# Laying out q and k of 14 attention chunks in DRAM for 32x32 turns on VectorE, with stores on SyncE's queue and GpSimd's long sums in halves

## The chip, the cores and the metric

The kernel runs on one core of one Trainium2 chip. Its time is the device time of one execution in microseconds (us); the figure to be predicted is the median of several runs. A core has five engines with an instruction stream each: TensorE (PE in the profile; its weight loads, PEld, are listed apart), VectorE (DVE), ScalarE (ACT), GpSimd (POOL) and SyncE (SP), which here only issues transfers. Transfers are carried out by 16 DMA engines, which serve a queue of SyncE (q1 in the profile) and one of ScalarE (q10).

## The reference

A linear attention with decay over blocks of the sequence, and after it a dense mixture of four two-layer networks. All is fp32.

```python
B, H, S, D = 4, 8, 768, 64            # q, k, v: (B, H, S, D)
for b in range(nb):                   # blocks of the sequence, kv_state starts at 0
    intra = einsum('bhic,bhjc->bhij', qb, kb) * Dmask
    intra = einsum('bhij,bhjd->bhid', intra, vb)
    inter = einsum('bhid,bhde->bhie', qb * lam_pow, kv_state)
    out[:, :, sl] = intra + inter
    kv_state = lam_block * kv_state + einsum('bhsd,bhse->bhde', kb * rev_pow, vb)
x = out.transpose(0, 2, 1, 3).reshape(B * S, H * D)       # (3072, 512)
p = domain_probs / (domain_probs.sum(-1, keepdims=True) + 1e-09)
for e in range(4):                    # w1: (4, 512, 1024), w2: (4, 1024, 512)
    h = maximum(x @ w1[e], 0.0)
    y += p[:, e:e + 1] * (h @ w2[e])
```

The kernel works in chunks of 128 positions: 6 for each of the 4 batches, 24 in all, numbered n = 0 to 23. The products of the mixture are cut in Strassen's way, with seven products (M1 to M7) where eight blocks would stand, on two levels; that takes sums and differences of blocks, which VectorE and GpSimd form.

## The kernel before

The scores need q and k with the feature on the partitions, and DRAM has them with the position on the partitions. A chunk is loaded in its natural layout, turned by TensorE against an identity, four transposes for q and four for k, and copied out of PSUM by ScalarE. VectorE scales q, GpSimd scales k in place once it is turned.

```python
def load(n, names="qkv"):
    b, c = divmod(n, NCH)                                   # NCH = 6 chunks in a batch
    for name in names:
        x = small(f"{name}n")                               # [128, 512], one of 47 buffers
        src = {"q": q, "k": k, "v": v}[name][b, :, c * C:(c + 1) * C, :]
        ...                                                 # q and k: two loads of 64 columns a head

def turn(n, tags):
    qn, kn = nat.pop((n, "q")), nat[n, "k"]
    qp, kp = bank(tags[0], "qp"), bank(tags[1], "kp")
    for x, y in ((qp, qn), (kp, kn)):
        for ac in range(NHP):                               # 4
            nc.tensor.transpose(out=x[:, ac * C:(ac + 1) * C], in_=y[:, 2 * ac:2 * ac + 2]..., identity=ident[:])
    qT, kT, qs = small("qT"), small("kT"), None
    nc.scalar.copy(out=qT[:], in_=qp[:])
    nc.scalar.copy(out=kT[:], in_=kp[:])
    if n % NCH:
        qs = small("qs")
        soon(n, lambda: tt(nc.vector, qs[:], qT[:], q_decay[:]..., ALU.mult))
    turned[n] = qT, kT, qs
    if n % NCH < NCH - 1:
        tt(nc.gpsimd, kd, kd, by.to_broadcast([P, NHP, 2, D]), ALU.mult)      # kd: kn, in place
```

`soon` puts small steps in front of a list of steps in the background, of which one is taken at each call of `rest()`. Chunks 0 to 7 are handled in an opening stage, the rest between the products of the mixture:

```python
for i in range(CPG + 2):                                    # opening: 8 chunks, first plain products
    ...
    for f, lag in ((scores, 1), (turn, 0), (values, 2)):
        ...
    if i + 4 < CPG:
        load(i + 4)
...
for at, (g, e) in enumerate(units):                         # 12 units: 3 groups of tokens, 4 experts
    for i in range(7):                                      # M1 .. M7
        ...
        for x, part in enumerate(order):                    # 8 parts: first product of the next unit,
            for f in part:                                  # second product of this one, in turns
                if f:
                    f()
            now[0] += 1
            ...
            rest()                                          # one step in the background
            if x == 0 and at * 7 + i >= 6 and fill:
                feed(*fill.pop(0))                          # loads xs_in, ws_in of a later product
            if steps and (at > 0 or i > 1) and (x == 5 or (x == 2 and i in (1, 3, 5) and at > 0)):
                steps.pop(0)()                              # turn, scores or values of one chunk
            if x % (2 if g == 0 else 3) == 0:
                pump()                                      # stores made before, then one chore
```

The operands of the products are summed by GpSimd, stored in DRAM and loaded again. Stores are issued by ScalarE, two pumps after they were noted:

```python
stores.append(lambda: (
    nc.scalar.dma_start(out=to[:, 0], in_=blk[:, 0, 0:256]),
    nc.scalar.dma_start(out=to[:, 1:5], in_=s[:]),
    nc.scalar.dma_start(out=to[:, 5:7], in_=blk[:, 1]...),
    made.add(what),
))

def total(name, a, b, op):                                  # of w1; w2 and x alike
    t = stage.tile([P, 2, W], FP32, name="w1o", tag="st")
    tt(nc.gpsimd, t[:], st[a][:], st[b][:], op)             # 1024 elements on each partition
    st[name] = t
```

Of the kernel before, what the change touches and what calls it, by code (L numbers as in the profile page):

```python
# [11 lines left out]
ALU = mybir.AluOpType  # L12
# [9 lines left out]
def kernel(  # L22
# [70 lines left out]
    def tt(eng, o, a, b, op):  # L93
        eng.tensor_tensor(out=o, in0=a, in1=b, op=op)  # L94


    nat = {}

    def load(n, names="qkv"):

        b, c = divmod(n, NCH)
        for name in names:
            x = small(f"{name}n")
            src = {"q": q, "k": k, "v": v}[name][b, :, c * C:(c + 1) * C, :]
            if name == "v":
                nc.sync.dma_start(out=x[:].rearrange("p (h d) -> p h d", d=D), in_=src.rearrange("h p d -> p h d"))
# [4 lines left out]
            nat[n, name] = x[:].rearrange("p (h d) -> p h d", d=D)  # L111

    lam_bc = consts.tile([P, H], FP32, name="lam_bc")
    nc.scalar.dma_start(out=lam_bc[:], in_=lam.partition_broadcast(P))
# [30 lines left out]
    def inner(eng, what, to, blk, ops, at):  # L145

        b = {n: blk[:, i, j * 256:(j + 1) * 256] for n, (i, j) in at.items()}
        s = stage.tile([P, 4, 256], FP32, name="ops", tag="st")
        for i, (name, x, y, op) in enumerate(ops):
            b[name] = s[:, SLOT[name]]  # L150
            tt(eng, b[name], b[x], b[y], op)
        stores.append(lambda: (
            nc.scalar.dma_start(out=to[:, 0], in_=blk[:, 0, 0:256]),
            nc.scalar.dma_start(out=to[:, 1:5], in_=s[:]),
            nc.scalar.dma_start(out=to[:, 5:7], in_=blk[:, 1].rearrange("p (a f) -> p a f", a=2)),
            made.add(what),
        ))

# [53 lines left out]
    def prepare_w2(e):  # L212
        st = {}

        def block(name, i, j):
            t = stage.tile([P, 2, 2, DH], FP32, name="w2b", tag="st")
            for uu in range(2):
                nc.sync.dma_start(out=t[:, uu], in_=w2_block(e, uu, i, j))
            st[name] = t

        def total(name, n, a, b, op):
            t = stage.tile([P, 2, 2, DH], FP32, name="w2o", tag="st")
            flat = [x[:].rearrange("p u c d -> p (u c d)") for x in (t, st[a], st[b])]
            tt(nc.gpsimd, *flat, op)
            stores.append(lambda: (
                nc.scalar.dma_start(out=w2_sums[e, n].rearrange("p u w -> p (u w)"), in_=flat[0]),
                made.add(("w2", e, name)),
            ))
# [32 lines left out]
    def prepare_w2_ops(e):  # L261
        st = {}

        def block(name, i, j):
            t = stage.tile([P, 2, 2, DH], FP32, name="w2b", tag="st")
            src = moe_w2[e, j * W:(j + 1) * W, i * DH:(i + 1) * DH]
            nc.sync.dma_start(out=t[:].rearrange("p q c d -> p (q c) d"), in_=src.rearrange("(k p) d -> p k d", p=P))
            st[name] = t

        def total(name, a, b, op):  # L270
            t = stage.tile([P, 2, 2, DH], FP32, name="w2o", tag="st")
            tt(nc.gpsimd, *(x[:].rearrange("p q c d -> p (q c d)") for x in (t, st[a], st[b])), op)
            st[name] = t

        return weight_steps(block, total, lambda m: inner_w2(e, m, st[A_OF[m]]))
# [8 lines left out]
    def prepare_x(g):  # L284

        st = {}

        def total(name, a, b, op):
            t = stage.tile([P, 2, W], FP32, name="xo", tag="st")
            tt(nc.gpsimd, t[:], a, b, op)  # L290
# [129 lines left out]
    def soon(n, *work):  # L420

        background[0:0] = work
        if n < CPG:
            rest(len(work))

    def turn(n, tags):
        qn, kn = nat.pop((n, "q")), nat[n, "k"]
        qp = bank(tags[0], "qp")
        kp = bank(tags[1], "kp")
        for x, y in ((qp, qn), (kp, kn)):  # L430
            for ac in range(NHP):
                nc.tensor.transpose(  # L432
                    out=x[:, ac * C:(ac + 1) * C], in_=y[:, 2 * ac:2 * ac + 2].rearrange("p r d -> p (r d)"),
                    identity=ident[:],
# [6 lines that stand above are left out]
            soon(n, lambda: tt(nc.vector, qs[:], qT[:], q_decay[:].rearrange("p h c -> p (h c)"), ALU.mult))  # L441
        turned[n] = qT, kT, qs
        if n % NCH < NCH - 1:

            kd = kn.rearrange("p (ac r) d -> p ac r d", r=2)
            by = k_decay.rearrange("p r ac -> p ac r").unsqueeze(3)
            tt(nc.gpsimd, kd, kd, by.to_broadcast([P, NHP, 2, D]), ALU.mult)

    def scores(n, tags):
        qT, kT, _ = turned[n]  # L450

        sp = [bank(tags[r], "sp") for r in range(2)]
# [57 lines left out]
    def attention(g):  # L510
# [3 lines left out]
        for n in range(g * CPG, (g + 1) * CPG):  # L514
# [3 lines left out]
            def end(n=n):  # L518
                values(n, ("s0", "s1"))
                if n + AHEAD < B * NCH:  # L520
                    load(n + AHEAD)
# [218 lines left out]
    def second_product(g, e, m, banks):  # L740

        def part(sj, s):
# [27 lines left out]
            else:  # L770
                nc.vector.scalar_tensor_tensor(out=o, in0=x, scalar=w, in1=o, op0=ALU.mult, op1=ALU.add)  # L771
            if e == E - 1 and m in ("M2", "M4", "M5", "M3"):
                stores.append(lambda: nc.scalar.dma_start(out=out[n * P:(n + 1) * P, j * DH:(j + 1) * DH], in_=o))

        def done():
            del fed2[g, e, m]
# [215 lines left out]
    def keep_own(what, to, pieces):  # L992
        def store():
            for (x, y), of in pieces:
                nc.scalar.dma_start(out=to[:, x:y], in_=of)
            made.add(what)

        stores.append(store)
# [47 lines left out]
    for i in range(CPG + 2):  # L1046
# [10 lines left out]
        for f, lag in ((scores, 1), (turn, 0), (values, 2)):  # L1057
# [16 lines left out]
    mine = {m: lambda m=m: own(m) for m in SEQ}  # L1074
    raws = [lambda n=n: raw_w1(1, n) for n in ("A11", "A12", "A21", "A22")]
    chores.extend((*prepare_w2(1), *raws, nothing, mine["M1"], lambda: sum_w1(1, "S1", "A21", "A22", ALU.add)))
    for m in SEQ0[2:]:
        for x, f in enumerate(direct_product(0, m, blocks, ("g1", "g3", "q01", "q02", "q11", "q12"))):
            f()
            rest()  # L1080
            if x < 4:
                pump()
    def sum_own(name, a, b):
# [14 lines left out]
    after_last = {"M2": (None,) * 5 + (("M3", 0), ("M3", 1)), "M4": (("M5", 0), ("M5", 1), ("M2", 0), ("M2", 1), ("M4", 0))}  # L1098
    steps = attention(1)
    for at, (g, e) in enumerate(units):  # L1100
        if (g, e) == (0, 1) or (g, e) == (0, 2):
            chores.extend(prepare_w2(e + 1) + prepare_w1((e + 2) % E))
        ahead = units[at + 1] if at + 1 < len(units) else None
# [9 lines left out]
        for i in range(7):  # L1113
# [27 lines left out]
            for x, part in enumerate(order):  # L1141
# [15 lines left out]
                        give(*y, ("s0", "s1"))  # L1157
                if x == 0 and at * 7 + i >= 6 and fill:
                    feed(*fill.pop(0))
                if at == 0 and x == 0 and i < AHEAD:  # L1160
# [35 lines left out]
```

## Time and profile before

The time is 1215.12 us, the median of 3 runs from 1214.82 to 1217.88 us. The profiled execution spans 1211.4 us at a granted TensorE clock of 0.999.

| what | value |
|---|---|
| q and k turned on TensorE (qp, kp) | 96 + 96 transposes of 128x128 |
| copies of qT and kT on ScalarE | 24 at 586 ns, 24 at 594 ns |
| q scaled on VectorE (qs) | 20 at 1184 ns |
| k scaled on GpSimd (kn) | 20 at 1074 ns |
| GpSimd sums of 128x1024 that the change cuts (w2o, w1o, xo) | 52, of 2.35 to 2.52 us in the mean of each group |
| loads of q and k, 128 KB each | 48 + 48, landing in 4.5 and 4.1 us |
| packets in all, bytes | 227446, 317.93 MB |
| packets under 512 B | 91648 |

The page of the profile has six parts: busy time of each engine; the same in 40 slices of the span; the DMA queues; the chain of work that ended last; the costliest groups of instructions, with idle time ahead of them and what ended it; the transfers. A matmul in fp32 stands as two records in the trace; a transpose as one. Matmuls overlap, and the mean duration of one is longer than the distance to the next.

### The profile page before, as it was taken

What the parts mean: (1) busy time and instruction counts of PE and PEld (TensorE: products, weight loads), DVE (VectorE), ACT (ScalarE), POOL (GpSimd) and SP (SyncE); (2) the same over time, 40 slices, a digit from 0 to 9 for tenths busy, and PEclk for the clock granted to TensorE, in tenths of its full rate; (3) what the DMA queues carried; (4) which work ended last, traced back from release to release, by engine and by line L of the source; (5) the groups of instructions that cost most, each with busy time, mean ns of one, the idle gap of its engine ahead of it and who ended that gap; (6) DMA issues with size and microseconds to landing.
All of it is one profiled execution on the core that took longest, in us unless ns stands there. A gap on an engine that the chain in (4) does not pass through costs nothing.

```text
span 1211.4 us, 17782 instructions
## 1 busy us (share of the span) xinstructions
PE 1186.9 (98%) x6593; PEld 1024.2 (85%) x6593; DVE 802.2 (66%) x1313; ACT 261.7 (22%) x476; POOL 622.8 (51%) x548
## 2 busy tenths in 40 slices
PE   7999999999999999999999999999999999999998
PEld 6788888888888888888888888888888888888877
DVE  5587686478567846746764874764665667777774
ACT  3322112112212211321211120120143241241132
POOL 4556247466366800015624655405665774873873
PEclk9999999999999999999999999999999999999999
DMA  9578489999999875679987998988986657566542
GB/s 234 155 274 270 168 279 316 367 311 317 350 338 320 282 264 188 221 246 292 293 288 239 293 315 318 333 288 258 326 301 235 238 202 268 198 258 209 204 170 74
DMA packets 227446, 317.93 MB, mean 262 GB/s; under 512 B 91648, under 2 KB 168864, under 8 KB 227360
## 3 DMA queue, kind: packets, MB, share of 16 engines
q1 hardware_dynamic: 191840, 257.08, 64.3%
q10 hardware_dynamic: 35520, 59.72, 13.4%
q8 instruction: 52, 0.85, 0.3%
q14 instruction: 34, 0.28, 0.1%
HBM read 231.40 MB, written 85.34 MB: 261 GB/s over the span
## 4 chain that ended last, share of the span: by engine, by line
PE 89%; DVE 5%; DMA 2%; SPq 1%; ACT 1%; issue 0%; POOL 0%; ACTq 0%; DVEq 0%
PE pg L701 38%; PE q L755 30%; PE pq L926 13%; DVE m L94 2%; PE sp L455 2%; PE op L483 2%; PE op L478 1%; PE pM L1016 1%; DVE hS L94 1%; DVE xt L94 1%; SPq L110 1%; PE kp L432 1%; PE op L491 1%; PE qp L432 1%; PE pM L896 1%
## 5 line engine op out<-in xcount | busy, mean ns | idle before, releaser
L701 PE MATMUL pg<-xs_in,ws_in 128*128 128x256 f32 x1960 | 473.7, 382 | 3.2 <-DVE m L94 2.5
L701 PEld LDWEIGHTS pg<-xs_in,ws_in 128*128 128x128 f32 x1960 | 367.4, 190 | 62.2 <-DVE m L94 9.9
L94 DVE TENSOR_TENSOR m<-pg,m 128x512 f32<-128x512 f32 x451 | 307.6, 688 | 134.1 <-PE pg L701 122.4
L755 PE MATMUL q<-w2t,hS 128*128 128x256 f32 x1024 | 242.5, 380 | 0.0
L755 PEld LDWEIGHTS q<-w2t,hS 128*128 128x128 f32 x1024 | 193.9, 190 | 26.7
L771 DVE SCALAR_TENSOR_TENSOR acc<-q,gate,acc 128x256 f32<-128x256 f32 x192 | 92.5, 482 | 147.6 <-PE q L755 147.1
L755 PE MATMUL q<-w2t,m 128*128 128x256 f32 x768 | 181.7, 379 | 0.0
L755 PEld LDWEIGHTS q<-w2t,m 128*128 128x128 f32 x768 | 145.4, 190 | 20.0
L713 ACT ACTIVATE m<-m 128x512 f32<-128x512 f32 x132 | 82.9, 632 | 348.2 <-DVE m L94 308.2
L94 POOL TENSOR_TENSOR kn<-kn,s_decay 128x512 f32<-128x512 f32 x20 | 21.5, 1074 | 204.7 <-PE kp L432 193.3
L94 POOL TENSOR_TENSOR m<-m,xT 128x512 f32<-128x512 f32 x64 | 81.2, 1288 | 73.9 <-ACT m L713 52.3
L94 DVE TENSOR_TENSOR sums<-pq,sums 128x256 f32<-128x256 f32 x154 | 64.6, 422 | 46.8 <-PE pq L926 41.9
L926 PE MATMUL pq<-acc,w2t 128*128 128x256 f32 x352 | 86.6, 379 | 0.0
L94 DVE TENSOR_TENSOR m<-m,m 128x512 f32<-128x512 f32 x96 | 84.6, 887 | 0.0
L709 ACT COPY m<-pg 128x512 f32<-128x512 f32 x88 | 51.0, 587 | 141.9 <-PE pg L701 128.9
L926 PEld LDWEIGHTS pq<-acc,w2t 128*128 128x128 f32 x352 | 66.7, 190 | 9.6 <-issue 0.6
L94 POOL TENSOR_TENSOR ops<-w2b 128x256 f32<-128x256 f32 x24 | 17.4, 745 | 98.3 <-DMA w2b<-in_moe_w_dram 66.9
L648 ACT ACTIVATE m<-m 128x512 f32<-128x512 f32 x48 | 30.4, 632 | 149.0 <-DVE m L94 149.0
L94 POOL TENSOR_TENSOR acc<-hT,hT 128x512 f32<-128x512 f32 x32 | 40.2, 1271 | 30.8 <-PE pq L926 21.4
L94 DVE TENSOR_TENSOR hS<-m,m 128x512 f32<-128x512 f32 x64 | 49.6, 779 | 5.6 <-ACT m L713 5.6
L94 POOL TENSOR_TENSOR w2o<-w2b 128x1024 f32<-128x1024 f32 x16 | 39.6, 2480 | 19.2 <-DMA w2b<-in_moe_w_dram 9.6
L94 POOL TENSOR_TENSOR ops<-w1o 128x256 f32<-128x256 f32 x32 | 29.7, 947 | 30.1 <-PE pg L701 20.5
(126 smaller groups left out, 1328.4 us busy)
## 6 DMA issues: line engine op xcount, KB each, us to landing
xs_in<-x_ops SPq DMA_DIRECT2D x70, 896.0 KB, 5.0
ws_in<-w_ops SPq DMA_DIRECT2D x70, 896.0 KB, 8.1
w2t<-w_ops SPq DMA_DIRECT2D x66, 256.0 KB, 6.9
w2t<-w_sums SPq DMA_DIRECT2D x64, 256.0 KB, 5.2
w_ops<-ops ACTq DMA_DIRECT2D x28, 512.0 KB, 5.5
w2t<-in_moe_w_dram SPq DMA_DIRECT2D x48, 256.0 KB, 5.0
x_ops<-ops ACTq DMA_DIRECT2D x17, 512.0 KB, 7.8
w2b<-in_moe_w_dram SPq DMA_DIRECT2D x32, 256.0 KB, 5.9
```

The costliest lines, as they stand in the source:

```text
L94: eng.tensor_tensor(out=o, in0=a, in1=b, op=op)
L110: nc.sync.dma_start(out=to[:, :, r], in_=of[:, :, r])
L432: nc.tensor.transpose(out=x[:, ac * C:(ac + 1) * C], in_=y[:, 2 * ac:2 * ac + 2].rearrange("p r d -> p (r d)"), identity=ident[:],)
L455: nc.tensor.matmul(out=sp[r][:, ac * C:(ac + 1) * C], lhsT=hc(kT)[half[r], ac], rhs=hc(qT)[half[r], ac], start=True, stop=True,)
L483: nc.tensor.matmul(out=op[r][half[x], a * C:(a + 1) * C], lhsT=vn[:, 4 * r + 2 * a + x], rhs=hc(st[r])[:, 2 * a + x], start=(first and a = ...
L648: nc.scalar.activation(out=o[:], in_=o[:], func=AF.Relu)
L701: nc.tensor.matmul(out=p[:, j * 256:(j + 1) * 256], lhsT=ws[i][:, j * P:(j + 1) * P], rhs=xs[i], start=(fresh and j == 0), stop=True, skip ...
L709: nc.scalar.copy(out=new[at][:], in_=p[:])
L713: nc.scalar.activation(out=new[at][:], in_=new[at][:], func=AF.Relu)
L755: nc.tensor.matmul(out=p[:, s * DH:(s + 1) * DH], lhsT=h[A_OF[m]][:, c * 256 + s * P:c * 256 + (s + 1) * P], rhs=fed2[g, e, m][uu][:, c], ...
L771: nc.vector.scalar_tensor_tensor(out=o, in0=x, scalar=w, in1=o, op0=ALU.mult, op1=ALU.add)
L926: nc.tensor.matmul(out=p[:, 0:256], lhsT=fed3[e, m, x // 2][:, x % 2, c * P:(c + 1) * P], rhs=b[B_OF[i]][:, c * 256:(c + 1) * 256], start= ...
```

## The change

For 14 chunks (chunks 2 to 5 of batch 1, all of batch 2, chunks 2 to 5 of batch 3) q and k are first copied from DRAM to DRAM into a tensor `across`, in runs of 32 columns, so that a load brings every 32x32 block to the partitions it belongs on, with its inside still unturned. VectorE then turns all blocks of such a tile in one instruction, in place. TensorE and ScalarE have no part in it. k is loaded in its natural layout too, as the update of the state needs it. Each batch takes 32 copies, a few issued at a time (`trickle`) in three stretches: behind the opening's loads, from the end of the opening into the first unit, and in the fourth unit (at = 3). All of the operand stores of ScalarE, and the stores of the output there, go to SyncE, and each of GpSimd's sums of 1024 elements becomes two of 512.

```diff
+    def halves(o, a, b, op):
+        for i in range(2):
+            tt(nc.gpsimd, o[:, i], a[:, i], b[:, i], op)
...
+    ACROSS = {1: 2, 2: 0, 3: 2}
+    across = dram.tile([B, 2, P, NHP, NCH * 4, 32], FP32, name="across")
+    def bring_across(b):
+        c = ACROSS[b]
+        for x, of in enumerate((q, k)):
+            for y in range(4):
+                for ac in range(NHP):
+                    src = of[b, 4 * (y // 2) + ac, c * C:, (y % 2) * 32:(y % 2 + 1) * 32]
+                    to = across[b, x, y * 32:(y + 1) * 32, ac, c * 4:]
+                    pieces.append(lambda to=to, src=src: nc.sync.dma_start(
+                        out=to, in_=src.rearrange("(t p) d -> p t d", p=32),
+                    ))
...
+    def load_across(n):
+        b, c = divmod(n, NCH)
+        for x, name in enumerate("qk"):
+            t = small(f"{name}x")
+            nc.sync.dma_start(
+                out=t[:].rearrange("p (h c) -> p h c", c=C),
+                in_=across[b, x, :, :, c * 4:c * 4 + 4].rearrange("p h t d -> p h (t d)"),
+            )
+            nat[n, name + "x"] = t
+    def load_more(n):
+        if not comes_across(n):
+            load(n)
+        else:
+            load_across(n)
+            load(n, "kv")
...
-            nc.scalar.dma_start(out=to[:, 0], in_=blk[:, 0, 0:256]),     # and so for every store
+            nc.sync.dma_start(out=to[:, 0], in_=blk[:, 0, 0:256]),
...
-            tt(nc.gpsimd, t[:], st[a][:], st[b][:], op)                  # and so in w2 and x
+            halves(t[:], st[a][:], st[b][:], op)
...
+    def turn_across(n):
+        qT, kT, kn = nat.pop((n, "qx")), nat.pop((n, "kx")), nat[n, "k"]
+        qs = small("qs") if n % NCH else None
+        def scaled():
+            if n % NCH:
+                tt(nc.vector, qs[:], qT[:], q_decay[:].rearrange("p h c -> p (h c)"), ALU.mult)
+            turned[n] = qT, kT, qs
+        soon(n, *(lambda x=x: nc.vector.transpose(out=x[:], in_=x[:]) for x in (qT, kT)), scaled)
+        if n % NCH < NCH - 1:
+            decayed(kn)                       # GpSimd scales k, as before
+    def turn(n, tags):
+        if comes_across(n):
+            turn_across(n)
+            return
...
     def scores(n, tags):
+        while n not in turned:
+            rest(force=True)
...
+            if i > 3:                         # opening, after each of its three steps
+                trickle(2)
+        if i == 3:
+            bring_across(1)
...
+    bring_across(2)                           # end of the opening; then one in two steps
+        if at == 3:
+            bring_across(3)
...
+                if at > 0 or i > 0:           # eight times in each product of a unit
+                    trickle()
                 if at == 0 and x == 0 and i < AHEAD:
-                    load(CPG + i)
+                    load_more(CPG + i)
```

More of the change, by code (lines that the diff above doesn't have):

```diff
@@ L111, in load, with trickle, comes_across @@
             nat[n, name] = x[:].rearrange("p (h d) -> p h d", d=D)
+    ACROSS = {1: 2, 2: 0, 3: 2}
+    across = dram.tile([B, 2, P, NHP, NCH * 4, 32], FP32, name="across")
+    pieces = []
+    def bring_across(b):
[8 more added lines that the diff above has]
+                    ))
+    def trickle(m=1):
+        for _ in range(m):
+            if pieces:
+                pieces.pop(0)()
+    def comes_across(n):
+        b, c = divmod(n, NCH)
+        return b in ACROSS and c >= ACROSS[b]
+    def load_across(n):
+        b, c = divmod(n, NCH)
+        for x, name in enumerate("qk"):
[11 more added lines that the diff above has]
+            load(n, "kv")
     lam_bc = consts.tile([P, H], FP32, name="lam_bc")
@@ L152, in inner @@
         stores.append(lambda: (
-            nc.scalar.dma_start(out=to[:, 0], in_=blk[:, 0, 0:256]),
-            nc.scalar.dma_start(out=to[:, 1:5], in_=s[:]),
-            nc.scalar.dma_start(out=to[:, 5:7], in_=blk[:, 1].rearrange("p (a f) -> p a f", a=2)),
+            nc.sync.dma_start(out=to[:, 0], in_=blk[:, 0, 0:256]),
+            nc.sync.dma_start(out=to[:, 1:5], in_=s[:]),
+            nc.sync.dma_start(out=to[:, 5:7], in_=blk[:, 1].rearrange("p (a f) -> p a f", a=2)),
             made.add(what),
@@ L223, in total @@
             flat = [x[:].rearrange("p u c d -> p (u c d)") for x in (t, st[a], st[b])]
-            tt(nc.gpsimd, *flat, op)
+            halves(*(x[:].rearrange("p u c d -> p u (c d)") for x in (t, st[a], st[b])), op)
             stores.append(lambda: (
-                nc.scalar.dma_start(out=w2_sums[e, n].rearrange("p u w -> p (u w)"), in_=flat[0]),
+                nc.sync.dma_start(out=w2_sums[e, n].rearrange("p u w -> p (u w)"), in_=flat[0]),
                 made.add(("w2", e, name)),
@@ L271, in total @@
             t = stage.tile([P, 2, 2, DH], FP32, name="w2o", tag="st")
-            tt(nc.gpsimd, *(x[:].rearrange("p q c d -> p (q c d)") for x in (t, st[a], st[b])), op)
+            halves(*(x[:].rearrange("p q c d -> p q (c d)") for x in (t, st[a], st[b])), op)
             st[name] = t
@@ L289, in total @@
             t = stage.tile([P, 2, W], FP32, name="xo", tag="st")
-            tt(nc.gpsimd, t[:], a, b, op)
+            halves(t[:], a, b, op)
             st[name] = t[:]
@@ L424, in soon, with decayed @@
             rest(len(work))
+    def turn_across(n):
[8 more added lines that the diff above has]
+            decayed(kn)
+    def decayed(kn):
+        kd = kn.rearrange("p (ac r) d -> p ac r d", r=2)
+        by = k_decay.rearrange("p r ac -> p ac r").unsqueeze(3)
+        tt(nc.gpsimd, kd, kd, by.to_broadcast([P, NHP, 2, D]), ALU.mult)
     def turn(n, tags):
+        if comes_across(n):
+            turn_across(n)
+            return
         qn, kn = nat.pop((n, "q")), nat[n, "k"]
@@ L443, in turn @@
         if n % NCH < NCH - 1:
-            kd = kn.rearrange("p (ac r) d -> p ac r d", r=2)
-            by = k_decay.rearrange("p r ac -> p ac r").unsqueeze(3)
-            tt(nc.gpsimd, kd, kd, by.to_broadcast([P, NHP, 2, D]), ALU.mult)
+            decayed(kn)
     def scores(n, tags):
+        while n not in turned:
+            rest(force=True)
         qT, kT, _ = turned[n]
@@ L520, in end @@
                 if n + AHEAD < B * NCH:
-                    load(n + AHEAD)
+                    load_more(n + AHEAD)
                 if n == g * CPG + CPG // 2 - 1:
@@ L772, in part @@
             if e == E - 1 and m in ("M2", "M4", "M5", "M3"):
-                stores.append(lambda: nc.scalar.dma_start(out=out[n * P:(n + 1) * P, j * DH:(j + 1) * DH], in_=o))
+                stores.append(lambda: nc.sync.dma_start(out=out[n * P:(n + 1) * P, j * DH:(j + 1) * DH], in_=o))
         def done():
@@ L994, in store @@
             for (x, y), of in pieces:
-                nc.scalar.dma_start(out=to[:, x:y], in_=of)
+                nc.sync.dma_start(out=to[:, x:y], in_=of)
             made.add(what)
@@ L1080 @@
             rest()
+            if x % 2:
+                trickle()
             if x < 4:
@@ L1159 @@
                     feed(*fill.pop(0))
+                if at > 0 or i > 0:
+                    trickle()
                 if at == 0 and x == 0 and i < AHEAD:
-                    load(CPG + i)
+                    load_more(CPG + i)
                 if steps and (at > 0 or i > 1) and (x == 5 or (x == 2 and i in (1, 3, 5) and at > 0)):
```

## The prediction, made before the run

> **What bounds the kernel now.** I read the busy times first, then the chain that ended last, then TensorE's own waits, and last the timeline around a turn. The page of the kernel before opens with:
>
> ```profile
> PE 1186.9 (98%) x6593; PEld 1024.2 (85%) x6593; DVE 802.2 (66%) x1313; ACT 261.7 (22%) x476; POOL 622.8 (51%) x548
> ...
> PE 89%; DVE 5%; DMA 2%; SPq 1%; ACT 1%; issue 0%; POOL 0%; ACTq 0%; DVEq 0%
> ```
>
> TensorE is busy for 98% of the span and carries 89% of the chain. So time goes down only by taking work from TensorE or closing its gaps; the gaps are 1211.4 - 1186.9 = 24.5 us. What each turned chunk costs is read from the timeline in the middle of the run:
>
> ```profile
> 313.17 1.89 PE L755 MATMUL q<-w2t,m 128*128 128x256 f32 x8
> 314.90 0.60 PE L432 MATMUL qp<-ident,qn 128*128 128x128 f32 x4
> 315.33 0.60 PE L432 MATMUL kp<-ident,kn 128*128 128x128 f32 x4
> 315.77 1.03 PE L701 MATMUL pg<-xs_in,ws_in 128*128 128x256 f32 x4
> 316.64 1.89 PE L755 MATMUL q<-w2t,m 128*128 128x256 f32 x8
> ```
>
> The columns are start, duration, instruction. The eight transposes lie between 314.90 and 315.77: 0.87 us, with no gap on either side. The chunk turned at 178.56 gives the same (179.43 - 178.56). The durations overlap, so the sum of durations (8 x 273 ns) would mislead; the distance of starts counts. Nothing else of TensorE's time hangs on a turn here. TensorE's waits by what ended them:
>
> ```profile
> PE qp L432 <- DMA qn<-in_q_dram: 6.2, 2, 4.5
> PE pg L701 <- DVE m L94: 4.8, 6, 1.7
> PE pg L701 <- ACT m L709: 2.8, 2, 2.1
> ```
>
> The first (6.2 us in total) is the start, where the change alters nothing: the first eight chunks keep their transposes. The two others, 7.6 us in 8 waits, can be touched. The cause of two kinds is visible in the timeline, first around 244 us:
>
> ```profile
> 244.02 2.34 POOL L94 TENSOR_TENSOR w1o<-w1b 128x1024 f32<-128x1024 f32 x1
> 244.31 2.60 DVE L94 TENSOR_TENSOR m<-m,m 128x512 f32<-128x512 f32 x1
> ...
> 247.57 1.99 PE L701 MATMUL pg<-xs_in,ws_in 128*128 128x256 f32 x8 [0.37 <-DVE m L94]
> ```
>
> A VectorE sum of two SBUF tiles, 0.68 us when alone (as at 278.60 us), takes 2.60 us because a long GpSimd sum started just ahead of it, and TensorE then stands for 0.37 us. Then around 98 us:
>
> ```profile
> 97.47 0.58 ACTq L995 DMA_DIRECT2D w_ops<-ops  x1
> 98.09 0.48 ACTq L995 DMA_DIRECT2D w_ops<-w1b  x1
> 98.61 1.15 ACT L1028 ACTIVATE m<-m 128x512 f32<-128x512 f32 x2 [2.68 <-DMA x_ops<-ops]
> ...
> 99.67 1.05 ACT L709 COPY m<-pg 128x512 f32<-128x512 f32 x2
> ```
>
> ScalarE issues six stores from 95.30 to 98.57 and only then copies the bank that TensorE needs back; TensorE's gap behind it is 2.14 us.
>
> [...] a bank of PSUM as one input escapes it (0.69 us throughout). A turn in place has one input, so it should not be held.
> [...] No such instruction is in this trace. A sum of 128x512 [...] I take its free duration, 0.68 us, as an estimate for one turn.
> [...] in the first 10 us q1 moved 7100 packets of 1.77 MB in 78.4% of 160 engine-us, 17.7 ns for 249 B, 14 B/ns; over the whole run its 191840 packets of 1340 B took 65 ns, 21 B/ns.
> [...] That is what ScalarE gets: 195 stores of its queue move, at 0.33 to 0.72 us each where I looked.
>
> **The change part by part.**
> Transposes: 14 chunks x 0.87 us = 12.2 us of TensorE's own stream removed, all on the path. That is 1.0% of 1215.
> ScalarE: 28 copies x 0.59 = 16.5 us removed, and the issue of stores. It is busy for 22%, so this counts only where TensorE waited for it: the waits of 2.14 and 0.64 us behind a string of stores. A gap costs about 0.35 us more than shown, as the weight load's own gap is longer (2.52 against 2.14). I book 3 us.
> GpSimd in halves: 52 sums become 104 of some 1.28 us (the row of 128x512 sums). GpSimd gains about 52 x 0.1 = 5 us of work, beside the path at 51% busy. A held VectorE sum then waits about 1.2 us at most rather than 2.3. Gaps in which a long sum stands just ahead are at 247.6, 278.1, 410.4 and 668.8 (0.37, 0.41, 1.42, 0.29), with 0.35 each 3.9 us. Two thirds of it are closed, I assume: 2.6 us.
> VectorE: 28 turns x 0.68 = 19 us added to 802. The stretches of 30 us between 210 and 660 us have it busy for 13 to 25 us, and a chunk comes each 30 us with 1.4 us more. It lies beside TensorE; a bank that is read out 0.68 us later may cost a little. I book 1 us lost.
> k's scaling: GpSimd waits 193.3 us in all for the turn of k. For the 14 chunks that wait goes, as the natural k is no longer an operand of TensorE. GpSimd then runs ahead, which helps the operands of the products, and changes which VectorE sums collide; no figure booked.
> DMA: 32 copies of 512, 768 and 512 rows make 57344 packets of 128 B. The 14 loads of q in 256 B rows (14336 packets) go; the 28 loads from the new layout are 14336 packets of 512 B. Taking 13 to 30 ns for a packet of 128 B (below the 17.7 ns, or well above it [...]), 57344 packets are 47 to 108 us of all 16 engines, over three stretches. Share before:
>
> ```profile
> 90.00:120.00 30.00, 27.86 (x129) 24.09 (x129) 24.45 (x38) 6.31 (x11) 18.92 (x18) 1.00 0.82 263
> 120.00:150.00 30.00, 30.00 (x155) 26.22 (x154) 19.50 (x36) 3.54 (x6) 6.71 (x8) 1.00 0.47 161
> ...
> 300.00:330.00 30.00, 30.00 (x178) 25.87 (x177) 13.91 (x23) 7.31 (x14) 8.09 (x4) 1.00 1.04 370
> ...
> 420.00:450.00 30.00, 30.00 (x192) 25.96 (x191) 13.16 (x23) 4.76 (x9) 4.33 (x5) 1.00 0.92 318
> 450.00:480.00 30.00, 30.00 (x178) 25.83 (x177) 19.70 (x34) 4.25 (x8) 0.00 (x0) 1.00 0.57 189
> ```
>
> The last two columns are the DMA share and GB/s, the second column TensorE's busy time. At 300 to 330 us the DMA engines are full and TensorE has no gap, so a full DMA isn't by itself a stop: operands are loaded one product (13 us) ahead and land in 5 to 8 us. The copies lie in 30 to 60 us (share 0.60), mostly 110 to 150 (0.47) and, as group 1's first turn is at 420.88 in unit 3, from about 403 to 460 (0.80 to 0.92, then 0.57). The second and third may push loads back by some us. I book 3 us lost for that and for SyncE, whose loads now queue behind stores that wait for GpSimd.
> Sum: 1215.1 - 12.2 - 3 - 2.6 + 1 + 3 = 1201.3 us.
>
> **The rivals.**
> First: DMA becomes the bound. For it: some windows have a share of 0.9 to 1.04 already, one queue has to carry what two did, and copies of 128 B are the costliest form. Against it: the copies stand where the share is lower, and from 160 to 400 us none is left but the loads. It would make 1205 to 1225.
> Second: SyncE's order. A store that waits for a late GpSimd sum holds up the loads after it. For it: SyncE waited 17.0 us for w2o sums at line 218, and 31.1 us for a free buffer at line 195. Against it: stores come two pumps (some 6 us) after the sum was asked for, and GpSimd has no wait for k's turn any more. It would add 3 to 10 us: 1204 to 1211.
> Third: the smoothing is worth more than I book, as all waits of 7.6 us go and the many short weight-load waits for VectorE (12.0 us in 22) with them: about 1193.
> Fourth: VectorE comes to pace the scores, as turn, turn and scaling stand in the background list one by one, and masks follow. From turn to scores there are at least three parts of 1.7 us, so that the forced steps are rare; +1 to 3 us.
>
> **Range and chances.** The removed 12.2 us are nearly certain; closing of gaps is bounded by about 10 us more, losses by the DMA have the longer tail. I say 1201 us, 8 in 10 between 1194 and 1212. 2% faster is 1190.8 us, below what all gaps of the middle would give; 2% slower is 1239.4 us, some 36 us over the sum, which needs DMA to become the bound in a long stretch. Chances: faster 0.04, within 2% 0.92, slower 0.04.
>
> **What would show it.** TensorE's rows qp and kp have 40 records each instead of 96, and its busy time is about 12 us lower with a share that stays at 98%. VectorE shows 28 transposes near 0.68 us; longer ones (over 1 us) would mean that they are held or go at half pace. ScalarE's queue q10 keeps almost nothing. The waits of TensorE for `ACT m L709` vanish and those for `DVE m` shrink. Packets rise by some 57000. The prediction is wrong if TensorE shows waits on xs_in, ws_in or w2t, if SyncE's waits on GpSimd grow by tens of us, if the share of DMA stays at 1 for longer than 60 us behind the copies, or if gaps appear ahead of the scores.

## The result, and the profile after

The changed kernel takes 1215.88 us, the median of 6 runs from 1212.59 to 1217.15; beside it the kernel before took 1215.52 (6 runs, 1212.97 to 1220.06). The ratio is 0.9994, with a 95% interval from 0.9971 to 1.0016: no difference. The prediction was 1201, between 1194 and 1212, so the time lies outside its range.

The page of the profile after, busy times and chain of work that ended last:

```profile
PE 1179.9 (97%) x6481; PEld 1019.6 (84%) x6481; DVE 810.1 (67%) x1341; ACT 247.2 (20%) x448; POOL 633.8 (52%) x600
...
PE 83%; DMA 6%; SPq 6%; DVE 2%; POOL 1%; issue 1%; ACT 0%; POOLq 0%; DVEq 0%
```

TensorE has the 112 instructions less that were asked for, but its share of the chain went from 89 to 83%, and what came in is DMA (2 to 6%) and SyncE's issuing (1 to 6%). TensorE's waits after, by what ended them (total, times, longest):

```profile
PE pg L771 <- DMA ws_in<-w_ops: 8.5, 3, 5.9
PE q L825 <- DMA w2t<-in_moe_w_dram: 8.2, 1, 8.2
PE qp L503 <- DMA qn<-in_q_dram: 6.2, 2, 4.5
PE pg L771 <- DVE m L94: 1.6, 2, 1.2
```

The wait for the start (6.2) is unchanged. Waits on VectorE fell from 4.8 to 1.6 us, and those on ScalarE's copy (2.8) are gone. In their place stand 16.7 us of waits for two loads, which had none before: the early weights w2t and the product's operand ws_in.

The two profiled executions (spans 1211.4 and 1215.4, clock 0.999 and 0.991) can be settled term by term. TensorE's gaps, span less busy time, went from 24.5 to 35.5: +11.0, of which +16.7 are the new waits and -6.0 the old ones. Its busy time fell by 7.0, not by 12.2: 5.2 us came back as the same matmuls took longer. (The granted clock is half for 3.4 us in the opening, and over the first 4.5 and 4.4 us of work behind the two longest of the new waits; in the kernel before it is full up to the last 2 us.) 11.0 - 7.0 = +4.0, the difference of the spans. The medians differ by only 0.4: the profiled execution of the kernel before is among its shorter ones, that of the changed kernel is the longest of its six.

Where it happens is seen by lining up the start of each chunk's scores in the two traces. The offset (after less before) is +1.9 us at 30 us; +9.3 for chunk 8 at 147 us; then it falls by 2.0 and 1.8, to +5.4 at 225 us (each time one turned chunk, and short waits of the kernel before that are smaller or gone); rises to +12.2 at 256; and falls again, at 555, 585, 616 and 646 us through 7.71, 6.83, 5.95 and 5.07, with no other event between. So a turned chunk brings its 0.87 us, and two places, about 100 and about 235 us, take it all back.

The first place. In the kernel before, SyncE issues the four loads of the first unit's w2t, and later operands, and TensorE uses them, as follows:

```profile
81.86 3.29 SPq L736 DMA_DIRECT2D w2t<-in_moe_w_dram  x4
...
96.34 1.89 PE L755 MATMUL q<-w2t,m 128*128 128x256 f32 x8
...
215.49 0.38 SPq L628 DMA_DIRECT2D xs_in<-x_ops  x1
215.93 0.45 SPq L630 DMA_DIRECT2D ws_in<-w_ops  x1
...
228.35 1.89 PE L701 MATMUL pg<-xs_in,ws_in 128*128 128x256 f32 x8
```

In the kernel after, TensorE and SyncE about 100 us:

```profile
97.29 1.10 PE L771 MATMUL pg<-ops 128*128 128x256 f32 x4
...
100.62 0.86 SPq L131 DMA_DIRECT2D across<-in_q_dram  x1
101.52 2.48 SPq L806 DMA_DIRECT2D w2t<-in_moe_w_dram  x4
...
106.56 3.75 PE L825 MATMUL q<-w2t,m 128*128 128x256 f32 x8 [8.17 <-DMA w2t<-in_moe_w_dram]
```

The load was issued at 81.86 and is now issued at 101.52, 19.7 us later; TensorE was ready at about 98.4 and stands for 8.17 us. The eight matmuls behind the wait then take 3.75 us where the same ones take 1.89, at a granted clock of 0.50.

The second place, the same kernel about 230 us:

```profile
216.91 0.32 SPq L202 DMA_DIRECT2D w_ops<-ops  x1
217.28 0.43 SPq L203 DMA_DIRECT2D w_ops<-w1o  x1
217.77 3.56 SPq L266 DMA_DIRECT2D w2b<-in_moe_w_dram  x4
...
228.78 1.26 SPq L806 DMA_DIRECT2D w2t<-w_sums  x2
230.13 0.44 SPq L698 DMA_DIRECT2D xs_in<-x_ops  x1
230.62 0.42 SPq L700 DMA_DIRECT2D ws_in<-w_ops  x1
...
239.82 3.75 PE L771 MATMUL pg<-xs_in,ws_in 128*128 128x256 f32 x8 [5.87 <-DMA ws_in<-w_ops]
```

SyncE stands from 213.6 to 216.9 at a store whose sum GpSimd has not finished, the last of four such stands that take 12.7 us together from 190 us on. Then it issues the weights w2b, which in the kernel before went out at 202.52, a chunk and three more stores, and comes to the operands of the next product at 230.13. In the kernel before ws_in went out at 215.93, 12.4 us ahead of its product; here it goes out at 230.62, 3.3 us ahead of the moment TensorE wants it (233.95), and takes 9.1 us to land. SyncE's waits for the sums at line 202 are 21.6 us in 9 over the run.

### The profile page after: what moved, and what is told of

The parts are those of the page before. It is cut to its first block, busy times and chain, and to the rows that moved or that the text cites. A ratio compares the mean times of both kernels' runs of the same rounds, so it can differ in the third digit from the quotient of the medians.

```text
span 1215.4 us, 17726 instructions
## 1 busy us (share of the span) xinstructions
PE 1179.9 (97%) x6481; PEld 1019.6 (84%) x6481; DVE 810.1 (67%) x1341; ACT 247.2 (20%) x448; POOL 633.8 (52%) x600
## 4 chain that ended last, share of the span: by engine, by line
PE 83%; DMA 6%; SPq 6%; DVE 2%; POOL 1%; issue 1%; ACT 0%; POOLq 0%; DVEq 0%
PE pg L771 36%; PE q L825 29%; PE pq L996 13%; DMA ws_in<-w_ops 2%; SPq L131 2%; SPq L115 1%; DMA w_ops<-ops 1%; PE op L553 1%; PE sp L525 1%; DMA w1b<-in_moe_w_dram 1%; DVE m L94 1%; DMA w_ops<-w1o 1%; SPq L266 1%; PE op L548 1%; SPq L367 1%
## 5 line engine op out<-in xcount | busy, mean ns | idle before, releaser
L94 POOL TENSOR_TENSOR kn<-kn,s_decay 128x512 f32<-128x512 f32 x20 | 22.7, 1137 | 111.1 <-PE kp L503 55.7
L94 POOL TENSOR_TENSOR w2o<-w2b 128x512 f32<-128x512 f32 x32 | 42.4, 1349 | 56.0 <-DMA w2b<-in_moe_w_dram 49.7
L94 POOL TENSOR_TENSOR acc<-hT,acc 128x512 f32<-128x512 f32 x32 | 40.7, 1271 | 7.4 <-PE pq L996 5.4
```

## The experiments

All ratios are against the kernel before, run beside the experiment on the same chip. Two theories (1 and 2 in the expectations). The first, call it order: everything now goes through SyncE's one queue in program order, so loads that TensorE needs are issued later, behind copies and behind stores that wait. The second, call it load: the 57344 packets of 128 B fill the DMA engines, and transfers land later, wherever they are issued.

**e1_across_only: the layout alone, stores on ScalarE and long sums whole, as before.**

```diff
-            nc.sync.dma_start(out=to[:, 0], in_=blk[:, 0, 0:256]),      # and so for every store
+            nc.scalar.dma_start(out=to[:, 0], in_=blk[:, 0, 0:256]),
-            halves(t[:], st[a][:], st[b][:], op)
+            tt(nc.gpsimd, t[:], st[a][:], st[b][:], op)
```

> The 32-column layout alone: stores go back to ScalarE's queue, GpSimd's sums stay whole. Theory 1 (order of SyncE's queue: the copies of the opening stand ahead of the weight loads, the stores ahead of the loads of unit 1): TensorE still waits 6 to 9 us for w2t near 98 us, but not for ws_in near 234 us; about 1209 to 1213 us. Theory 2 (the DMA engines are filled by packets of 128 B, whoever issues): both waits stay, as the packets are the same; 1215 to 1219 us.

Measured: 1235.72 us, ratio 1.016 (1.0139 to 1.0180). Slower by 20 us, above what either theory gave, so the rest of the change is not decoration (of its two parts it is the stores that count, as e6 shows). ScalarE in this trace:

```profile
103.17 0.36 ACTq L1064 DMA_DIRECT2D w_ops<-w1b  x1
105.65 0.33 ACTq L1064 DMA_DIRECT2D w_ops<-ops  x1
107.19 0.33 ACTq L1064 DMA_DIRECT2D w_ops<-w1b  x1
107.57 1.15 ACT L1097 ACTIVATE m<-m 128x512 f32<-128x512 f32 x2 [7.02 <-DMA w_ops<-w1b]
```

The same six stores, which the kernel before issued in 3.3 us, take 7.6 us while the DRAM copies are in flight (99.92 to 107.52), and the work of ScalarE behind them, among it copies out of PSUM, is late. w2t is late too (issued at 103.11).

**e2_stores_only: the kernel before, with its stores on SyncE.** The reverse edit of the first two lines above, for every store, and nothing else.

> The kernel before with the stores on SyncE and nothing else; no copies. Theory 1: no wait for w2t near 98 us, but a wait of some us for ws_in near 234 us, with slow matmuls behind it; the waits for ScalarE's copies go; 1216 to 1221 us. Theory 2: no new wait at all, about 1212 us.

Measured: 1215.73 us, 0.9995 (0.9984 to 1.0006). The stores alone delay the early w2t from 81.86 to 97.06 us, and that costs a wait of 2.0 us, with 1.6 us more in matmuls at a lower clock behind it; the waits on ScalarE go, as in the full change, and the sum is nothing. Neither expectation was met: w2t does wait, and ws_in doesn't. So SyncE's order takes up all the slack of w2t at hardly a loss. In the full change the load goes out 4.5 us later still (101.52; 4.0 of it go with the copies, as e4 below has 97.52), lands 1.1 us more slowly, and TensorE is there 0.6 us sooner: 6.2 us more of waiting, 8.2 in place of 2.0.

**e4_no_copies: everything but the copies.** The loads of the turned chunks read q and k directly in runs of 512 B, so that all other work is the same; the scores are then made of other values.

```diff
-                in_=across[b, x, :, :, c * 4:c * 4 + 4].rearrange("p h t d -> p h (t d)"),
+                in_=(q, k)[x][b].rearrange("h s d -> (h s d)").rearrange("(p h x) -> p h x", p=P, h=NHP)[:, :, c * C:(c + 1) * C],
     def bring_across(b):
+        return
```

> The changed kernel without the 96 copies from DRAM to DRAM; qx and kx are loaded with the same 512 B runs straight from q and k, so blocks hold the wrong values, and all else is as changed. Theory 1: the wait for w2t goes (10 us with the slow matmuls behind it), the one for ws_in near 234 us stays in part; 1203 to 1207 us. Theory 2: both go; 1197 to 1201 us.

Measured: 1204.26 us, 0.9907 (0.9888 to 0.9926). Without copies most of the predicted gain is there. Waits of 1.6 us (w2t) and 3.2 us (ws_in) are left, with the stores on SyncE and no copies: theory 1's expectation.

**e9_long_runs: the same number of copies and of bytes, in runs of 2 to 3 KB.** The turned chunks read what that leaves, so again other values.

```diff
-                    src = of[b, 4 * (y // 2) + ac, c * C:, (y % 2) * 32:(y % 2 + 1) * 32]
+                    m = (S - c * C) * 32
+                    src = of[b, 4 * (y // 2) + ac].rearrange("s d -> (s d)")[(y % 2) * m:(y % 2 + 1) * m]
...
```

> The changed kernel with the same 96 copies, bytes and places in the queue, but in runs of 2 to 3 KB instead of 128 B (32 packets a copy instead of 512 or 768); the values land in the wrong places. Theory 1: the copies still stand ahead of the weight loads, so a wait for w2t of at least 4 us stays; 1208 to 1214 us. Theory 2: the packets are gone, both waits go; 1198 to 1203 us.

Measured: 1210.06 us, 0.9949 (0.9933 to 0.9965), with waits of 2.6 us (w2t) and 6.5 (ws_in) and, at the opening, 2.3 us on ScalarE that the change itself doesn't show: there a load that ScalarE issues, of the probabilities, holds up its stream for 6.2 us. The time is what theory 1 gave; the wait for w2t, at least 4 us by it, is not.

**e6_stores_back: the layout and the halves, stores on ScalarE.** It differs from e1 by the halves alone.

> The changed kernel with the stores back on ScalarE: layout and halves, no move of stores. Against the layout alone (1235.7 us) it shows what the halves are worth. If held VectorE sums are a small part: 1232 to 1236 us; if they are the reason of the waits for ScalarE and VectorE there: below 1225 us.

Measured: 1232.88 us, 1.0142 (1.0125 to 1.0159), beside 1.016 of e1. TensorE's waits for VectorE's `m` fall from 6.3 to 4.7 us. By the medians the halves are worth some 0.2%, and the intervals overlap.

**e10_short_copies: as many copies, of 32 rows each, with e4's loads.** It leaves the issuing and removes bytes and packets.

```diff
-                    src = of[b, 4 * (y // 2) + ac, c * C:, (y % 2) * 32:(y % 2 + 1) * 32]
+                    src = of[b, 4 * (y // 2) + ac, c * C:c * C + 32, (y % 2) * 32:(y % 2 + 1) * 32]
```

> The changed kernel with 96 copies in the same places of the queue, each of 32 packets of 128 B only, and with qx and kx loaded from q and k as in the run without copies (wrong values): what is left is the place in the queue and the time to issue. If the issue of 96 transfers costs the time: 1209 to 1213 us. If packets and bytes cost it: 1204 to 1206 us, as without copies.

Measured: 1214.25 us, 0.9985 (0.9975 to 0.9995), which looks as if issuing were all. The trace says otherwise; ScalarE in the opening:

```profile
49.52 0.40 ACTq L1142 DMA_DIRECT2D probs<-in_moe_domain_probs_dram  x1
50.01 0.59 ACT L1094 COPY m<-pM 128x512 f32<-128x512 f32 x1 [11.07 <-DMA across<-in_q_dram]
```

ScalarE did nothing for some 11 us ahead of its load of the probabilities, until, by the trace, one of SyncE's copies had landed, and the copies out of PSUM stood behind it. That is a loss which the change doesn't have there, so this run doesn't tell the theories apart. e17 below repeats it with that load moved.

**e11_early_w2t: the change, with the first unit's w2t loads issued some 24 us earlier.**

```diff
     for m in SEQ0[2:]:
+        if m == "M7":
+            feed2(0, 0, "M1"); feed2(0, 0, "M2")
```

> The changed kernel with the four loads of w2t for the first unit, which depend on nothing, put into SyncE's queue some 20 us earlier, ahead of the stores of x_ops and w_ops that stand in front of them now; nothing is left out. Theory 3 (the stores on SyncE take 15 us of slack from w2t, the copies 4 to 5 us more, and only the sum exceeds the slack): the wait near 98 us goes with its slow matmuls, 1203 to 1208 us, as low as without any copies. Theory 2 (the DMA engines are full): the loads only take the place of others, the wait moves to another operand; 1212 to 1216 us.

Measured: 1211.07 us, 0.9953 (0.9924 to 0.9981). Issued at 77.23, the load has no wait and no slow matmuls behind it: the first place was a matter of its issue alone. The time lies between the two expectations, as the second place takes the gain: the offset is -6.0 us at 225 us, but +1.5 at 256.

```profile
PE pg L771 <- DMA ws_in<-w_ops: 9.1, 4, 6.4
```

e4, e7 and e11, in which SyncE carries the stores, begin the scores of chunk 10 at 222.6, 221.7 and 218.6 us and yet those of chunk 11 all at 256.5 to 257.5; e2, which comes to chunk 10 at 227.2, gets there at 257.5 without a wait for ws_in. In the first three ws_in goes out at 219.4 to 220.3 whatever TensorE's lead, so something other than TensorE sets the pace of this stretch.

**e7_clean_opening: ten chunks only (none of batch 1), the copies of batch 2 inside the first unit.** `ACROSS = {2: 0, 3: 2}`.

> The changed kernel with 10 chunks instead of 14: batch 1 stays as before, and the copies of batch 2 begin in the first unit, so the opening issues no copy. Theory 3: w2t is issued near 97 us, the wait there is 1 to 3 us instead of 8.2, and 4 x 0.87 us of turns come back; 1207 to 1211 us. Theory 2: the copies of batch 2 now all meet the operand loads of unit 0, waits appear between 115 and 160 us; 1213 to 1218 us.

Measured: 1209.04 us, 0.9947 (0.9924 to 0.9971). w2t is issued at 93.91 with a wait of 1.5 us; ws_in waits 4.4. Fewer gains, fewer losses.

**e12_early_later: e11, and each store three pumps after it was noted instead of two.** The sums have longer to be done before SyncE comes to the store.

```diff
-        for f in older:
+        for f in oldest:
             f()
+        oldest[:] = older
```

> The kernel with the early loads of w2t, and every store issued one pump later (three after it was noted instead of two), nothing left out. Theory 4 (in unit 1 SyncE stands at stores whose GpSimd sums are not done, near 203 to 207 us, and so issues xs_in and ws_in late): the wait for ws_in near 230 us is gone or under 2 us; 1202 to 1206 us. Rival 5 (from 205 to 390 us the DMA engines are full, and what TensorE gains before is given back there): the wait stays at 3 to 7 us; 1208 to 1213 us.

Measured: 1206.23 us, 0.9922 (0.9905 to 0.9938). ws_in waits once, for 2.2 us, where e11 waited 9.1; VectorE's `m` rises to 5.4. It isn't shown that the later stores did it: at the second place ws_in goes out at 220.49, in e11 at 219.41, and the wait is shorter because TensorE, held for 3.8 us by `m` near 107 us, comes 5.6 us later. The intervals of e11 and e12 overlap too.

**e13_early_pool: e11, with GpSimd issuing the operand stores.** `nc.sync` becomes `nc.gpsimd` in these stores; they then follow their sums in GpSimd's own order, and SyncE has none of them to wait at.

> The kernel with the early loads of w2t, and the operand stores issued by GpSimd, which makes the sums, so that neither SyncE nor ScalarE waits for them. Theory 4: no wait of SyncE for GpSimd and none of TensorE for ws_in near 230 us, if the issue doesn't make GpSimd itself late; 1202 to 1208 us. Rival 5: the wait for ws_in stays; 1209 to 1216 us.

Measured: 1218.43 us, 1.0018 (1.0006 to 1.0030), with ws_in waiting 18.6 us. In this trace each issue takes GpSimd about 0.55 us, and GpSimd's sums themselves come late: SyncE now stands 12.0 us at once for a w1o sum, at a load of weights (line 243). It shows that this cure is worse, outside both expectations; of the theories it tells nothing.

**e14_clean_early and e15_clean_early_later: ten chunks with the early w2t, and that with the later stores.** They join the edits of e7, e11 and, for e15, e12.

> 10 chunks with no copy in the opening, and the early loads of w2t. Theory 4 and rival 5 alike: the 1.5 us wait near 98 us goes too, but TensorE arrives the earlier at the wait of unit 1, which grows by as much (3.6 to some 5 us); the same as with the clean opening alone, 1206 to 1209 us.

> 10 chunks with no copy in the opening, early loads of w2t and stores one pump later: the version that should beat both kernels. Theory 4: no wait near 98 us, none over 2 us near 230 us; 1201 to 1205 us. Rival 5: 1206 to 1210 us.

Measured: e14 1206.01 us, 0.9920 (0.9900 to 0.9939), ws_in 4.4; e15 1203.54 us, 0.9901 (0.9883 to 0.9920). The stores' place is the only difference between them. In e14 ws_in goes out at 220.39 and TensorE waits 4.1 us; in e15 it goes out at 215.87, as in the kernel before (215.93), TensorE waits 0.5 us, and the offset stays: -3.9 us ahead of the second place, -3.8 behind it. SyncE stands for GpSimd's `ops` sums as long in both (11.0 and 10.9 us from 190 to 235 us); what has changed is that each load has one group of stores less ahead of it. e15 loses 5.4 us elsewhere, about 450 us, where the copies of batch 3 run (one wait for ws_in is 3.2 us), so that the medians differ by 2.5 us only and the intervals overlap.

**e17, e18, e19: the ladder of the copies.** All three are the full change with the probabilities' load moved ahead of the copies (`if i == 3` for `if i == 5`). e17_short_probs has e10's short copies, e18_long_probs e9's long runs, e19_full_probs the copies of the change.

> As the short copies (96 copies of 32 packets of 128 B; qx and kx loaded from q and k, wrong values), with the load of the probabilities issued before the copies. If the issue and the place in the queue cost nothing much: 1203 to 1206 us, as without copies. If they cost the time: 1209 to 1213 us.

> As the long runs (same bytes, 32 packets of 2 to 3 KB a copy, values in the wrong places), with the load of the probabilities before the copies. If packets alone cost the time: 1203 to 1206 us; if bytes do: 1209 us and more; between them if both.

> The changed kernel with the load of the probabilities before the copies and nothing else changed: the reference for the short and the long copies. In the changed kernel that load was not held up, so the same as it within 0.3%: 1213 to 1218 us.

| kernel | issuing | bytes | short packets | us | ratio and interval |
|---|---|---|---|---|---|
| e4 | no | no | no | 1204.26 | 0.9907 (0.9888 to 0.9926) |
| e17 | yes | no | 3072 | 1206.88 | 0.9915 (0.9888 to 0.9942) |
| e18 | yes | yes | no | 1209.26 | 0.9934 (0.9910 to 0.9958) |
| e19 | yes | yes | 57344 | 1215.43 | 1.0000 (0.9985 to 1.0015) |

From e18 to e19 only the cutting into packets of 128 B differs, and the step of 6 to 8 us (by medians or by ratios) is beyond the intervals; e9 beside the change itself gives 5 to 6. The steps before it can't be priced. In all three kernels the moved load still holds up ScalarE, by the trace now behind the loads of the opening (9.5, 11.0 and 11.1 us), and TensorE waits 2.9 to 3.6 us for a copy of ScalarE behind it, which neither e4 nor the change does. In e19:

```profile
31.30 0.59 ACT L1094 COPY m<-pM 128x512 f32<-128x512 f32 x1 [11.08 <-DMA vn<-in_v_dram]
...
32.91 2.08 PE L525 MATMUL sp<-qT,kT 64*128 64x128 f32 x16 [3.58 <-ACT kT L509]
```

So the 1 to 3 us from e4 to e17 are not the price of issuing, and the 2 us from e17 to e18 lie within the intervals. Of the 7.0 us between the traces of e18 and e19 3.2 arise in the opening, where the clock falls behind this wait in e19 alone. That e19 is no slower than the change, in spite of its opening, is because TensorE is later at the first place and waits less there (w2t 3.7 us, ws_in 7.4).

Both theories hold a part: with packets of 2 to 3 KB the copies of e9 still cost 5 to 6 us over e4, some of it by ScalarE's load, and the short packets cost as much again or more. At the second place ws_in goes out at 220.34 us in e4, 222.80 in e17, 224.98 in e18 and 229.79 in e19; but from e18 to e19 TensorE comes later by as much (4.7 us), so that these times don't tell which of the two holds up the other.

**e20_best_slower: e15, with the copies of batch 3 issued in six of eight parts of a product.**

```diff
-                if at > 0 or i > 0:
+                if (at > 0 or i > 0) and (at < 3 or x % 4 < 3):
```

> The best version so far (10 chunks, early loads of w2t, stores one pump later; 1203.5 us) with the copies of batch 3 issued in six of eight parts instead of all eight. If they cause the wait of 3 us for ws_in near 455 us by coming too dense: that wait is halved or gone, 1200 to 1203 us. If not: 1203 to 1205 us.

Measured: 1202.54 us, 0.9882 (0.9852 to 0.9912): the lowest median of all, not to be told from e15 by the intervals, and faster than both kernels. The wait of 3.2 us that e15 has about 450 us is gone. TensorE's waits (there is no row of w2t):

```profile
PE pg L772 <- DVE m L94: 1.8, 3, 1.2
PE pg L772 <- DMA ws_in<-w_ops: 1.8, 3, 1.4
```

And the window of the second place, in the view by windows (second column TensorE's busy time, the last three its clock, the DMA share and GB/s), first the kernel after:

```profile
225.00:240.00 15.00, 9.13 (x53) 7.52 (x52) 6.52 (x11) 0.58 (x1) 2.50 (x2) 0.91 1.02 322
```

then e20:

```profile
225.00:240.00 15.00, 14.76 (x106) 12.44 (x106) 7.25 (x12) 0.74 (x2) 7.42 (x6) 1.00 1.04 406
```

The DMA engines are full in both (share 1.02 and 1.04). TensorE stands for 5.9 us in one and 0.24 in the other. A full DMA is then not enough to make this wait; with the load issued as early as before, it is carried.

## Why the prediction was wrong

**Right.** The 112 transposes came off TensorE at 0.87 us a chunk: the offset falls by 0.87 or 0.88 with each of the four chunks from 555 to 646 us. That a turn takes as long as a free sum of 128x512 (0.68 us) was the author's estimate, and VectorE's groups bear it out:

```profile
L484 DVE STREAM_TRANSPOSE qx<-qx 128x512 f32<-128x512 f32 x14 | 9.8, 701 | 0.0
L484 DVE STREAM_TRANSPOSE kx<-kx 128x512 f32<-128x512 f32 x14 | 9.8, 700 | 0.0
```

None of the 28 was held (689 to 702 ns each, 17 of them with a GpSimd sum beside them), as had been expected from their having one input. The trace of the kernel before had shown this for the 451 sums `m<-pg,m`, whose other input is in PSUM: 673 to 693 ns, where a sum of two SBUF tiles beside a GpSimd sum took up to 2.84 us. The 5.6 us booked for smoothing measured 6.0: ScalarE's waits -2.8, VectorE's -3.2. GpSimd's wait for the turn of k fell from 193.3 to 55.7 us; its busy time rose by 11.0 us, where 5 had been expected. No gap came ahead of the scores, so the fourth rival fell; the third, more smoothing, did too.

**The step that failed** is "I book 3 us lost for that and for SyncE". The two waits measured 16.7 us, and the matmuls behind them, at half clock, cost some 4 us more, for which the sum had no term: 20 to 22 in place of 3. (The rest of the 5.2 us that came back is the half clock in the opening.) Waits on ws_in and w2t are what the prediction itself named as signs of its being wrong. The mistake was to weigh the DMA by its share ("a full DMA isn't by itself a stop") and by stretches, and never to ask of each load how much later it may go out. The trace of the kernel before held the figure: the first w2t was issued at 81.86, landed at 90.19 and was used at 96.34. So 6.2 us were to spare, or some 10 where it lands in 3.8 to 4.9 us, as it later did in e2 and in the change. The stores on SyncE took 15.2 (e2), and TensorE was 2.6 us later there by itself; the change took 4.5 more. The first shift used up the slack at small cost, the second then counted in full.

**The second rival** (SyncE's order, 1204 to 1211) was right in kind and counted too small, and the argument held against it, that stores come two pumps after their sum was asked for, was wrong: two pumps were not enough, as SyncE waited 21.6 us for these sums, and with one pump more the load goes out 4.5 us earlier and its wait at that place falls from 4.1 to 0.5 us (e14, e15). **The first rival** (DMA as the bound, 1205 to 1225) had the result within its range and the costliest form right: 6 to 8 us hang on the short packets (e18, e19). The packets' own price was in the range given: between 36 and 43 us 5271 packets of q1, 142 B in the mean, took 62.0% of 112 engine-us, 13.2 ns each, where 13 to 30 had been taken. They act through loads that have no slack left; a full DMA alone was no bound at the second place (e20). (A slip without effect: 1239.4 us lies 38 us over the predicted sum, not 36.)

**The issue of stores.** ScalarE's gain was booked as 3 us on top. It is instead what makes the copies bearable: with the stores on ScalarE the layout costs 1.6% (e1). In e1 six issues took 7.6 us in place of 3.3, and the engine's own work stood behind them.

**Open.** How much of the pace between 225 and 256 us is SyncE's waiting at stores, and how much the issues themselves (12.9 us from the first w2b to ws_in), was not separated: e15 changes what stands ahead of the load but not the length of the waiting, e18 and e19 change the copies, and each moves the wait. Removing the waiting alone wasn't tried. Nor is it known what holds ScalarE's load of the probabilities in e9, e10 and e17 to e19 and not in the change. At 20 to 30 us the granted clock in the profile after is 0.83, which costs 1.6 us, though TensorE's waits there (1.68 and 0.22 us) are those of the kernel before (1.71 and 0.25), which kept the full clock. The halves can't be told from nothing.

## What to carry to other kernels

Work taken off the engine that bounds a kernel pays only as far as its prefetched loads can go out earlier too; list for each load its issue, its landing and the moment it is needed, and check that slack against everything that the change puts ahead of it in the same issuing order, summed. Loads that depend on nothing go ahead of stores that wait for a sum. The copies in runs of 128 B took 13.2 ns of a DMA engine for each packet here, and cost 6 to 8 us more than as many bytes in runs of 2 to 3 KB (e18, e19); beside them ScalarE's six stores took 7.6 us to issue in place of 3.3, so an engine that issues transfers beside such copies should have no urgent work of its own behind them.

## What had not been expected of the hardware

A long wait of TensorE cost more than its length here. After waits of 8.17, 5.87 and 3.72 us (the kernel after and e19) the next eight matmuls took 3.75 us instead of 1.89. At 2.00 and 2.73 us it went either way; TensorE's timeline in e2, and then in e17:

```profile
100.98 3.51 PE L755 MATMUL q<-w2t,m 128*128 128x256 f32 x8 [2.00 <-DMA w2t<-in_moe_w_dram]
```

```profile
103.55 1.97 PE L825 MATMUL q<-w2t,m 128*128 128x256 f32 x8 [2.73 <-DMA w2t<-in_moe_w_dram]
```

The granted clock behind the first is 0.55 for 3.4 us, behind the second 1.00. Half clock lasted 3.4 us in e2, and 3.4, 10.2 and 6.8 us in the kernel after. TensorE had not stood for as long as that ahead of each fall: in e2 a wait of 2.0 us was enough, with two short ones (0.91 and 0.16 us) before it, and TensorE had been busy for 1.4 of the 3.4 us before the fall; in the opening of the kernel after it had been busy for 1.5. What sets the moment of a fall, and how long it lasts, is not shown. A fall cost 1.6 to 1.9 us in these eight matmuls beyond the wait, and where the half clock lasted longer some 0.4 in the next (2.31 us in place of 1.89 at 243.36).
